# Spectral and dense layers on one core: the first chunk's residual summed in PSUM by TensorE, in place of the last tile's

## The chip, the cores and the metric

The kernel runs on one core of a Trainium2 chip. The metric is the device time of one execution in microseconds (us), as the median of several runs. A core has five engines that run their own instruction streams and meet at semaphores: TensorE (PE, matmuls), VectorE (DVE), ScalarE (ACT), GpSimd (POOL) and SyncE (SP, here only an issuer of DMAs). TensorE reads SBUF and writes PSUM, which has 8 banks of 512 fp32 values per partition.

## What is computed

The reference applies two kinds of layer in turn, twice, each with a residual, to x of 2048 rows by 1024 columns in bf16:

```python
def _A_ref(x, w_r, w_i):
    B, S, D = x.shape
    X = rfft2(x.astype(jnp.float32), axes=(-2, -1))
    X = X * (w_r + 1j * w_i)
    return irfft2(X, s=(S, D), axes=(-2, -1)).astype(jnp.bfloat16)

def _B_ref(x, w1, b1, w2):
    h = jnp.einsum("bsd,df->bsf", x, w1) + b1
    sp = jnp.log1p(jnp.exp(-jnp.abs(h))) + jnp.where(h > 0, h, jnp.zeros_like(h))
    return jnp.einsum("bsf,fd->bsd", h * jnp.tanh(sp), w2)

x = A_x
x = x + _A_ref(_layernorm(x, axis=-1), A_w_r, A_w_i)
x = x + _B_ref(_layernorm(x, axis=-1), B_w1, B_b1, B_w2)
x = x + _A_ref(_layernorm(x, axis=-1), A_w_r, A_w_i)
x = x + _B_ref(_layernorm(x, axis=-1), B_w1, B_b1, B_w2)
```

S is 2048, D is 1024 and F, the inner width of the dense layer, is 3584. `_layernorm` subtracts the row's mean and divides by the root of its variance.

## The kernel before

**State.** The residual stream x stays in SBUF as `XS`, sixteen tiles of 128 rows by 1024 columns in bf16. `IDENT` is a 128x128 identity. The PSUM is one tensor `PS` of eight banks. A small planner in Python orders everything: `op`, `group` and `dma` put instructions on an engine's list and work out its waits from `Res` objects, one for each tile or bank. A reader waits for the writers, a writer for the writers and readers. The program order on each engine is the order of the calls. A `Res` after `begin()` takes writes to its parts, each of which waits only for what was there before. `copy` lists the bank that it reads among its writes, so it counts as a writer of it.

**Transform layer (`layer_A`).** The two-dimensional transform is done as chains of matmuls by tables (`s1`, `s2`, `s3`, then `i1`, `i2`), in eight groups. At the end each group's result goes to DRAM and comes back turned (`u_turn`, `u_back`, `u_last`) as `UT`, with a `Res` for each of four quarters of its 128 row slots. While the last rows come, TensorE runs `spin`, matmuls of width 512 whose result nobody reads (line 905, 26 of them on bank 0). `load_w1` then starts the six first blocks of the dense weights.

**Start of the dense layer (`layer_B`).** The transform's last step is a matmul for each row slot of `UT` with a slice of `MT` (`i4`, line 968). With `lo` 0 and `nb` 4 it gives tiles 0 to 3 (32 columns per slot, 16 slots to a bank), with `lo` 4 and `nb` 12 the other twelve tiles (96 columns per slot). `i4_out` takes the sums out of PSUM. At lines 1146 to 1151, for each quarter `u`: `i4` into banks 2u and 2u+1; VectorE adds tiles 0 and 1 to `XS` (line 990); ScalarE copies tiles 2 and 3 to a buffer `YC` (line 568); VectorE takes statistics of a quarter of tiles 0 and 1 (`stats_quarter`, lines 472 and 474). The other twelve tiles come in pieces of up to 15 slots (`rest`, copied to `YS`, mostly by ScalarE). Then `root` (ScalarE's root at line 432, VectorE's reciprocal at 434), `apply` (the normalisation, line 512), transposes on TensorE (line 1024) with VectorE's copy (line 1029), and the first product `mm1` with the activation Mish on ScalarE (lines 1058 and 1062). Tiles are taken in chunks of four, and the first chunk's `mm1` at first in halves of 256 rows, with `rest` pieces between (lines 1169 to 1175). `residual` (line 1137) adds `YC` to tiles 2 and 3 and `YS` to tiles 4 to 15, on VectorE.

**End of the dense layer.** `mm2` forms the second product, 28 matmuls for each half of a tile (line 1079), and VectorE adds it to `XS` (line 1087). In the first dense layer each finished tile is normalised at once for the second transform. Tiles 0 to 14 go through DRAM (`xn_store`, `xr_load`). Of tile 15 the second half is done otherwise: an identity matmul puts the residual into PSUM first (line 1077), the product is summed on top of it, and `finish_last` takes the statistics and normalises straight from PSUM, in two halves. `xr_direct` then moves the tile as sixteen DMAs, one for each half and column block, on SP, ScalarE and POOL in turn: rows 0 to 3 after the first half, 4 to 15 after the second. The matmuls of the next `s1` (line 629) wait for the first eight of them in half 0, and later for half 1. A spin of 24 fills the wait (line 1245).

Three lines that are easy to miss, the planner's rule in `copy` and the order of the queues:

```python
return self.op(prog, fn, reads=reads, writes=writes, parts=parts)
...
self.copy(prog or self.act, at(staged.ap), src, [], rb, parts=[staged.res])
...
prog = (self.sp, self.act, self.pool)[i % 3]
```

Of the kernel before, what the change touches and what calls it, by code (L numbers as in the profile page):

```python
# [7 lines left out]
P = 128  # L8
# [171 lines left out]
class KB:  # L180
# [352 lines left out]
    def xr_direct(self, j, b, rows):  # L533

        for i in rows:
            half, h = i // 8, i % 8
            n = slice(64 * half, 64 * half + 64)
            prog = (self.sp, self.act, self.pool)[i % 3]
            self.dma(prog, self.XR.ap[row_of(j, h):row_of(j, h) + 1, n, :], b.ap[n, h * P:(h + 1) * P], f"xd{half}{prog.name}",
                     reads=[b.res], parts=[self.r_xr[2 * half]])  # L540

    def finish_last(self, bank):


        j, dve, ps = 15, self.dve, self.PS[:, bank, :]
        rb, r = self.r_bank[bank], self.r_mv[15]
        self.op(dve, lambda e: e.bn_stats(self.BN[:, j, 6:12], ps), reads=[rb], parts=[r])
        self.op(dve, lambda e: e.bn_aggr(self.MV[:, j, :], self.BN[:, j, :]), reads=[r], writes=[r])
        self.root(j, 1)
        b = self.xn_out[0]  # L550
        assert not b.unread
        mean, rs = self.MV[:, j, 0:1], self.RS[:, 2, j:j + 1]
        b.res.begin()
        for h in range(2):
            src = ps if h else self.XS[:, j, 0:512]
            self.op(dve, lambda e, h=h, src=src: e.tensor_scalar(b.ap[:, 512 * h:512 * h + 512], src, mean, rs, op0=ALU.subtract, op1=ALU.mult),
                    reads=[rb if h else self.r_xs[j], r, self.r_rs[j]], parts=[b.res])
            self.xr_direct(j, b, range(4, 16) if h else range(4))
        self.copy(self.act, self.XS[:, j, 512:1024], ps, [], [rb, self.r_xs[j]])
# [125 lines left out]
    def layer_A(self, li):  # L685
# [219 lines left out]
        self.spin(26, 0)  # L905
# [55 lines left out]

    def i4(self, lo, nb, u0, n, bank):

        w = 8 * nb
        k = 512 // w
        fns = []
        for l in range(n):
            fns.append(lambda e, l=l: e.matmul(self.PS[:, bank + l // k, l % k * w:(l % k + 1) * w], self.UT.ap[:, u0 + l, :],  # L968
                                               self.MT[:, 8 * lo:8 * lo + w], start=True, stop=True))
        self.group(fns, reads=self.r_ut[u0 // 32:(u0 + n - 1) // 32 + 1] + [self.r_mt], writes=self.r_bank[bank:bank - (-n // k)])  # L970

    def i4_out(self, lo, nb, u0, n, bank, staged=None, prog=None, tiles=None):
# [3 lines left out]
        t0, tn = tiles or (0, nb)  # L976

        for b0, m, i in ((0, n // k, k), (n // k, 1, n % k)):
            if not m or not i:
                continue  # L980
            src = self.PS[:, bank + b0:bank + b0 + m, 0:i * w].rearrange("p b (i c) -> p c b i", c=w)[:, 8 * t0:8 * (t0 + tn)]
            l = slice(u0 + b0 * k, u0 + b0 * k + m * i)
            rb = self.r_bank[bank + b0:bank + b0 + m]

            def at(ap):
                return ap.rearrange("p n (h l) -> p (n h) l", l=P)[:, :, l].rearrange("p c (b i) -> p c b i", i=i)
            if staged is None:
                j = slice(lo + t0, lo + t0 + tn)
                xs = at(self.XS[:, j, :])
                self.op(self.dve, lambda e, src=src, xs=xs: e.tensor_tensor(xs, src, xs, ALU.add), reads=rb, parts=self.r_xs[j])  # L990
            else:

                self.copy(prog or self.act, at(staged.ap), src, [], rb, parts=[staged.res])
# [10 lines left out]
    def layer_B(self, li, last):  # L1004
# [63 lines left out]
        def mm2(c, t, h):  # L1068
# [5 lines left out]

            summed = not last and (j, h) == (15, 1)
            if summed:
                fns.append(lambda e: e.matmul(PS[:, bank, :], self.IDENT[:], self.XS[:, j, 512:1024], start=True, stop=False))
            for i, ft in enumerate(range(NF)):
                fns.append(lambda e, i=i, ft=ft: e.matmul(  # L1079
                    PS[:, bank, :], at.ap[:, ft, t * P:(t + 1) * P], W2[ft].ap[:, h * 512:(h + 1) * 512],  # L1080
                    start=(i == 0 and not summed), stop=(i == NF - 1)))
            self.group(fns, reads=ra + r_w2 + ([self.r_xs[j], self.r_ident] if summed else []), writes=[self.r_bank[bank]])
            if summed:
                self.finish_last(bank)
                return
# [9 lines left out]
            else:  # L1095
# [4 lines left out]
                self.xn_store(j, self.apply(j, out=True))  # L1100
# [13 lines left out]
        YC = self.alloc("YC", self.ob["XT1"], [2, self.D])  # L1114
        YC.res.begin()
        xn = {}
        for j in range(2):
            self.r_xs[j].begin()

# [15 lines left out]
        def residual(j):  # L1135
            y, i = (YS, j - 4) if j > 3 else (YC, j - 2)
            self.op(dve, lambda e: e.tensor_tensor(self.XS[:, j, :], self.XS[:, j, :], y.ap[:, i, :], ALU.add),
                    reads=[y.res], writes=[self.r_xs[j]])
# [7 lines left out]
        for u in range(4):  # L1146
            self.i4(0, 4, 32 * u, 32, 2 * u)
            self.i4_out(0, 4, 32 * u, 32, 2 * u, tiles=(0, 2))
            self.i4_out(0, 4, 32 * u, 32, 2 * u, staged=YC, tiles=(2, 2))
            for j in range(2):  # L1150
                self.stats_quarter(j, u)
        rest(0)
        self.root(0, 2)
# [3 lines left out]
        self.spin(6, 7)  # L1157
        for j in range(2):
            transposed(0, j, xn[j])
        rest(3)  # L1160
        self.warm(ACT.Mish)
        at_tiles(0)
        for j in (2, 3):
            residual(j)
# [4 lines left out]
        for fg in range(4):  # L1169
            mm1(0, fg, 0, mid=turns(0, 2, 3) if fg == 3 else ())  # L1170
            rest(3)
            if fg == 2:
                rest(6, 10, dve)
        mm1(0, 0, 1)
        rest(3, 13)
# [108 lines left out]
```

## Time and profile before

| quantity | value |
|---|---|
| median of 3 runs | 1019.48 us (1019.28 to 1019.52) |
| profiled execution, its own time | 1019.28 us |
| span of the profiled execution | 1017.5 us |
| mean granted TensorE clock | 0.996 |
| TensorE line 1079 (`mm2`), 1756 matmuls | 385.7 us busy, 379 ns each |
| TensorE line 1058 (`mm1`), 1950 matmuls | 389.3 us busy, 358 ns each |
| VectorE line 990 (add of tiles 0 and 1), 8 | 5.4 us busy, 678 ns each |
| VectorE line 472 (quarter statistics), 16 | 6.1 us busy, 413 ns each |
| ScalarE line 568 at 128x512, 8 | 4.8 us busy, 597 ns each |
| TensorE line 646 (spin), 84 | 18.9 us busy, 379 ns each |

Times inside the execution count from the first instruction of the span. A row's mean is the length of one instruction from start to end. Matmuls overlap, so a run of them takes less than count times mean: 24 spins of 379 ns took 5.34 us. In the chain of work that ended last, each piece is followed by what it released. "Idle before" names what an engine waited for. A granted clock of 0.5 means that TensorE ran at half rate.

### The profile page before, as it was taken

Reading aid. Unit: us, or ns where it says so; the run is one execution under the profiler, and the core shown is the slowest. Engines: PE = TensorE matmul, PEld = TensorE weight load, DVE = VectorE, ACT = ScalarE, POOL = GpSimd, SP = SyncE. Lnnn points to the kernel's source line nnn. Section 1 sums busy time; section 2 is a strip of 40 time slices with the busy share of each in tenths; the row PEclk is TensorE's granted clock in tenths of the full one; section 3 lists DMA queues with packets and bytes.
Section 4 is the critical chain, followed back from the end, with each engine's and each line's share of the span. In section 5 each row is a group of like instructions: output and inputs, shape, how many; then the busy total and the mean of one; then the engine's idle time right before and its main releaser. Section 6 shows DMA issues by size and latency. Waiting matters only on the chain.

```text
span 1017.5 us, 13734 instructions
## 1 busy us (share of the span) xinstructions
PE 956.8 (94%) x5780; PEld 507.8 (50%) x5866; DVE 327.8 (32%) x679; ACT 347.9 (34%) x483; POOL 81.5 (8%) x114
## 2 busy tenths in 40 slices
PE   0799799999999999999999978999999999999998
PEld 0577475444444444444446757644444444444443
DVE  6797469002344000033346836830011100000111
ACT  7798383430000344300019847543200024330000
POOL 4651000000000000002521100000000000000000
PEclk9999999999999999999999999999999999999999
DMA  9979823562111220001922974246411212100000
GB/s 285 244 221 319 209 64 108 178 211 74 46 46 33 73 83 21 1 21 72 207 63 74 241 187 134 91 159 206 127 26 46 74 52 75 50 1 11 21 26 27
DMA packets 154205, 107.00 MB, mean 105 GB/s; under 512 B 74448, under 2 KB 133664, under 8 KB 154144
## 3 DMA queue, kind: packets, MB, share of 16 engines
q1 hardware_dynamic: 143056, 78.61, 27.5%
q0 software_dynamic: 8912, 25.84, 8.9%
q10 hardware_dynamic: 2176, 1.66, 0.5%
q8 instruction: 47, 0.77, 0.3%
q14 instruction: 14, 0.11, 0.0%
HBM read 80.85 MB, written 20.71 MB: 100 GB/s over the span
## 4 chain that ended last, share of the span: by engine, by line
PE 86%; DMA 4%; DVE 3%; SPq 3%; ACT 3%; issue 1%; POOL 0%; ACTq 0%; DVEq 0%; POOLq 0%
PE PS L1079 38%; PE PS L1058 37%; SPq L249 3%; PE PS L789 2%; PE PS L715 2%; PE PS L810 2%; DMA ARENA<-in_A_w_i_dram 1%; PE PS L968 1%; DMA ARENA<-c_bt 1%; DMA ARENA<-u_scratch 1%; ACT ARENA L568 1%; PE PS L828 1%; PE PS L1024 1%; PE PS L761 1%; ACT ARENA L796 1%
## 5 line engine op out<-in xcount | busy, mean ns | idle before, releaser
L1058 PE MATMUL PS<-ARENA 128*128 128x512 bf16 (+1 forms) x1950 | 389.3, 358 | 2.5 <-DVE ARENA L1029 0.6
L1079 PE MATMUL PS<-ARENA 128*128 128x512 bf16 x1756 | 385.7, 379 | 1.9
L1062 ACT ACTIVATE ARENA<-PS,B 128x512 bf16<-128x512 f32 (+1 forms) x248 | 158.9, 645 | 410.9 <-PE PS L1058 410.6
L1058 PEld LDWEIGHTS PS<-ARENA 128*128 128x128 bf16 x1984 | 192.9, 98 | 193.7 <-DVE ARENA L1029 1.6
L1079 PEld LDWEIGHTS PS<-ARENA 128*128 128x128 bf16 x1792 | 175.3, 98 | 211.3
L1087 DVE TENSOR_TENSOR XS<-PS,XS 128x512 bf16<-128x512 f32 x63 | 43.6, 692 | 581.3 <-PE PS L1079 581.3
L460 DVE BATCH_NORM_STATS2 BN<-XS 128x6 f32<-128x512 bf16 x99 | 64.0, 675 | 6.0 <-DMA XS<-in_A_x_dram 4.8
L568 ACT ACTIVATE ARENA<-PS 128x1440 bf16<-128x1440 f32 (+3 forms) x26 | 28.0, 1095 | 28.4 <-DVE XS L990 24.8
L249 POOL DMA_DIRECT2D xn_scratch<-ARENA x12 | 6.5, 541 | 375.8 <-DVE ARENA L512 375.8
L789 PE MATMUL PS<-ARENA 128*128 128x256 bf16 x256 | 32.4, 273 | 4.1 <-DVE ARENA L778 3.2
L796 ACT ACTIVATE ARENA<-PS 128x1024 bf16<-128x1024 f32 x32 | 33.1, 1054 | 7.0 <-PE PS L789 7.0
L432 ACT ACTIVATE RS<-MV,EPS 128x2 f32<-128x2 f32 (+2 forms) x5 | 1.5, 298 | 97.4 <-DVE MV L463 84.4
L715 PE MATMUL PS<-FD,ARENA 128*128 128x256 bf16 (+1 forms) x256 | 31.8, 271 | 2.4 <-ACT ARENA L635 1.2
L767 ACT ACTIVATE ARENA<-PS 128x1024 bf16<-128x1024 f32 x32 | 32.5, 1044 | 4.5 <-PE PS L763 4.5
L789 PEld LDWEIGHTS PS<-ARENA 128*128 128x128 bf16 x256 | 24.3, 98 | 11.8 <-DVE ARENA L778 5.5
L771 DVE TENSOR_TENSOR ARENA<-ARENA 128x1024 bf16<-128x1024 bf16 x32 | 22.0, 689 | 20.4 <-ACT ARENA L767 20.3
L810 PE MATMUL PS<-ARENA,BD 128*128 128x256 bf16 x192 | 25.9, 280 | 2.3 <-ACT ARENA L796 2.3
L838 ACT ACTIVATE ARENA<-PS 128x1024 bf16<-128x1024 f32 x26 | 26.8, 1066 | 2.9 <-PE PS L810 2.9
L715 PEld LDWEIGHTS PS<-FD,ARENA 128*128 128x128 bf16 x256 | 24.4, 98 | 6.5 <-DVE ARENA L637 1.4
L512 DVE TENSOR_SCALAR ARENA<-XS,MV,RS 128x1024 bf16<-128x1024 bf16 x47 | 25.3, 563 | 0.9
L968 PE MATMUL PS<-MT,ARENA 128*128 128x32 bf16 (+1 forms) x512 | 21.2, 195 | 4.0 <-ACT ARENA L568 2.0
L750 ACT ACTIVATE ARENA<-PS 128x1024 bf16<-128x1024 f32 x22 | 22.9, 1058 | 3.1 <-PE PS L715 3.1
(83 smaller groups left out, 519.8 us busy)
## 6 DMA issues: line engine op xcount, KB each, us to landing
ARENA<-in_B_w_dram SPq DMA_DIRECT2D x56, 512.0 KB, 4.0
ARENA<-in_B_w_dram SPq DMA_DIRECT2D x56, 256.0 KB, 4.3
u_scratch<-ARENA SPq DMA_DIRECT2D x14, 512.0 KB, 3.7
ARENA<-u_scratch SPq DMA_DIRECT2D x14, 512.0 KB, 6.1
w_scratch<-ARENA POOLq DMA_DIRECT2D x8, 512.0 KB, 6.5
ARENA<-w_scratch POOLq DMA_DIRECT2D x8, 512.0 KB, 5.0
out_dram<-XS SPq DMA_DIRECT2D x16, 256.0 KB, 2.0
ARENA<-xn_scratch POOLq DMA_DIRECT2D x15, 256.0 KB, 9.5
```

Source lines behind the costliest of these rows:

```text
L249: return eng.dma_start(out_ap, in_ap).then_inc(ds.sem, 16)
L460: self.op(self.dve, lambda e: e.bn_stats(self.BN[:, j, 6 * h:6 * h + 6], self.XS[:, j, 512 * h:512 * h + 512]), reads=[self.r_xs[j]], part ...
L568: fn = (lambda e: e.activation(dst, src, ACT.Copy)) if scale is None else \
L715: fns.append(lambda e: e.matmul(dst, at(r), FD[:, t:t + n], start=start, stop=stop))
L767: self.op(act, lambda e: e.activation(x.ap.rearrange("p a b -> p (a b)"), ps, ACT.Copy, scale=SIG), reads=banks, writes=[x.res])
L789: fns.append(lambda e, c=c, part=part: e.matmul(ps[:, c * 256:(c + 1) * 256], yk.ap[:, part, c * P:(c + 1) * P], t[:, (128, 0)[part]:(384, ...
L796: self.op(act, lambda e: e.activation(v.ap[:, :, i, :], src, ACT.Copy), reads=banks, parts=[v.res])
L810: fns.append(lambda e, dst=dst, part=part, c=c: e.matmul(dst, BD[:, c:c + P], mov(kd, part), start=(part == 0), stop=(part == 1)))
L1058: fns.append(lambda e, db=db, bank=bank, fl=fl: e.matmul(PS[:, bank, 0:w], wb.ap[:, db, fl * P:(fl + 1) * P], x.ap[:, db, tok], start=(db ...
L1062: self.op(act, lambda e, bank=bank, ft=ft: e.activation(at.ap[:, ft, tok], PS[:, bank, 0:w], ACT.Mish, bias=self.B1[:, ft:ft + 1]), reads= ...
L1079: fns.append(lambda e, i=i, ft=ft: e.matmul(PS[:, bank, :], at.ap[:, ft, t * P:(t + 1) * P], W2[ft].ap[:, h * 512:(h + 1) * 512], start=(i ...
L1087: self.op(dve, lambda e: e.tensor_tensor(xs, PS[:, bank, :], xs, ALU.add), reads=[self.r_bank[bank]], writes=[self.r_xs[j]])
```

## The change

There are two parts. Tile 15 loses its own treatment: `finish_last` and the identity matmul go, its second half is added by VectorE and normalised as a whole like other tiles, and `xr_direct` issues all sixteen DMAs after that. The first chunk is given the identity matmul instead: `residual_first` puts `XS` of tiles 0 to 3 into the eight banks, with 8 identity matmuls of width 512, after a spin of 8 (before: a spin of 26). `i4` for these tiles then sums on top. ScalarE copies the sums of tiles 0 and 1 to `XS` (`out_first`), and VectorE takes only the statistics; the sums of tiles 2 and 3 follow, three copies on ScalarE and one on VectorE, ahead of the root in the program. `YC` and its two adds go, so does the spin of 6 on bank 7, and the `rest` pieces are dealt out anew: two before the normalisation, none between transposes and `mm1`, and three small ones on VectorE. Both dense layers have the change at their start; only the first had the tile 15 treatment.

```diff
--- before.py
+++ after.py
@@ -530,33 +530,15 @@
         self.dma(self.pool, self.XR.ap[row_of(j, 0):row_of(j, 7) + 1:4, :, :], self.xn_d[j].rearrange("n (h l) -> h n l", l=P), f"xl{j % 4}",
                  reads=[self.r_xnd[j]], parts=self.r_xr[1:3])
-    def xr_direct(self, j, b, rows):
-        for i in rows:
+    def xr_direct(self, j, b):
+        b.unread = False
+        for i in range(16):
             half, h = i // 8, i % 8
             n = slice(64 * half, 64 * half + 64)
             prog = (self.sp, self.act, self.pool)[i % 3]
             self.dma(prog, self.XR.ap[row_of(j, h):row_of(j, h) + 1, n, :], b.ap[n, h * P:(h + 1) * P], f"xd{half}{prog.name}",
                      reads=[b.res], parts=[self.r_xr[2 * half]])
-    def finish_last(self, bank):
-        j, dve, ps = 15, self.dve, self.PS[:, bank, :]
-        rb, r = self.r_bank[bank], self.r_mv[15]
-        self.op(dve, lambda e: e.bn_stats(self.BN[:, j, 6:12], ps), reads=[rb], parts=[r])
-        self.op(dve, lambda e: e.bn_aggr(self.MV[:, j, :], self.BN[:, j, :]), reads=[r], writes=[r])
-        self.root(j, 1)
-        b = self.xn_out[0]
-        assert not b.unread
-        mean, rs = self.MV[:, j, 0:1], self.RS[:, 2, j:j + 1]
-        b.res.begin()
-        for h in range(2):
-            src = ps if h else self.XS[:, j, 0:512]
-            self.op(dve, lambda e, h=h, src=src: e.tensor_scalar(b.ap[:, 512 * h:512 * h + 512], src, mean, rs, op0=ALU.subtract, op1=ALU.mult),
-                    reads=[rb if h else self.r_xs[j], r, self.r_rs[j]], parts=[b.res])
-            self.xr_direct(j, b, range(4, 16) if h else range(4))
-        self.copy(self.act, self.XS[:, j, 512:1024], ps, [], [rb, self.r_xs[j]])
     def pair(self):
         i = self.npair % 4
@@ -902,7 +884,8 @@
             else:
                 i2(g, h)
                 u_turn(g, h)
-        self.spin(26, 0)
+        self.spin(8, 0)
+        self.residual_first()
         if li == 0:
             self.op(self.pool, lambda e: e.tensor_copy(self.B1[:], self.B1h[:]), reads=[self.r_b1h], writes=[self.r_b1])
         self.w1_buf = [self.alloc(f"W1_{i}", (self.W1_OFF + i * 4096, 140 * K + (i - 4) * 4096)[i > 3], [8, 256]) for i in range(6)]
@@ -959,6 +942,16 @@
         i = 2 * g % 8
         self.dma(self.pool, self.w_d[g], self.wt_pair(i), f"ws{g % 4}", reads=[w.res for w in self.WT[i:i + 2]], writes=[self.r_wd[g]])
+    def residual_first(self):
+        for b in range(8):
+            out = self.PS[:, b, :].rearrange("p (l c) -> p c l", c=32)
+            xs = self.XS[:, 0:4, :].rearrange("p n (h l) -> p (n h) l", l=P)[:, :, 16 * b:16 * b + 16]
+            self.group([lambda e, out=out, xs=xs: e.matmul(out, self.IDENT[:], xs, start=True, stop=False)],
+                       reads=self.r_xs[0:4] + [self.r_ident], writes=[self.r_bank[b]])
+        for r in self.r_xs[0:4]:
+            r.begin()
     def i4(self, lo, nb, u0, n, bank):
         w = 8 * nb
@@ -966,31 +959,30 @@
         fns = []
         for l in range(n):
             fns.append(lambda e, l=l: e.matmul(self.PS[:, bank + l // k, l % k * w:(l % k + 1) * w], self.UT.ap[:, u0 + l, :],
-                                               self.MT[:, 8 * lo:8 * lo + w], start=True, stop=True))
+                                               self.MT[:, 8 * lo:8 * lo + w], start=lo > 0,
+                                               stop=lo > 0 or l % k == k - 1))
         self.group(fns, reads=self.r_ut[u0 // 32:(u0 + n - 1) // 32 + 1] + [self.r_mt], writes=self.r_bank[bank:bank - (-n // k)])
-    def i4_out(self, lo, nb, u0, n, bank, staged=None, prog=None, tiles=None):
+    def out_first(self, u, t, prog):
+        b = slice(2 * u, 2 * u + 2)
+        src = self.PS[:, b, :].rearrange("p b (i c) -> p c b i", c=32)[:, 8 * t:8 * t + 16]
+        dst = self.XS[:, t:t + 2, :].rearrange("p n (h l) -> p (n h) l", l=P)[:, :, 32 * u:32 * u + 32]
+        self.copy(prog, dst.rearrange("p c (b i) -> p c b i", i=16), src, [], self.r_bank[b], parts=self.r_xs[t:t + 2])
+    def i4_out(self, lo, nb, u0, n, bank, staged, prog):
         w = 8 * nb
         k = 512 // w
-        t0, tn = tiles or (0, nb)
         for b0, m, i in ((0, n // k, k), (n // k, 1, n % k)):
             if not m or not i:
                 continue
-            src = self.PS[:, bank + b0:bank + b0 + m, 0:i * w].rearrange("p b (i c) -> p c b i", c=w)[:, 8 * t0:8 * (t0 + tn)]
+            src = self.PS[:, bank + b0:bank + b0 + m, 0:i * w].rearrange("p b (i c) -> p c b i", c=w)
             l = slice(u0 + b0 * k, u0 + b0 * k + m * i)
-            rb = self.r_bank[bank + b0:bank + b0 + m]
-            def at(ap):
-                return ap.rearrange("p n (h l) -> p (n h) l", l=P)[:, :, l].rearrange("p c (b i) -> p c b i", i=i)
-            if staged is None:
-                j = slice(lo + t0, lo + t0 + tn)
-                xs = at(self.XS[:, j, :])
-                self.op(self.dve, lambda e, src=src, xs=xs: e.tensor_tensor(xs, src, xs, ALU.add), reads=rb, parts=self.r_xs[j])
-            else:
-                self.copy(prog or self.act, at(staged.ap), src, [], rb, parts=[staged.res])
+            dst = staged.ap.rearrange("p n (h l) -> p (n h) l", l=P)[:, :, l].rearrange("p c (b i) -> p c b i", i=i)
+            self.copy(prog, dst, src, [], self.r_bank[bank + b0:bank + b0 + m], parts=[staged.res])
     def load_w1(self, after=()):
@@ -1071,18 +1063,11 @@
             bank = 3 + no[0] % 3
             no[0] += 1
             fns = []
-            summed = not last and (j, h) == (15, 1)
-            if summed:
-                fns.append(lambda e: e.matmul(PS[:, bank, :], self.IDENT[:], self.XS[:, j, 512:1024], start=True, stop=False))
             for i, ft in enumerate(range(NF)):
                 fns.append(lambda e, i=i, ft=ft: e.matmul(
                     PS[:, bank, :], at.ap[:, ft, t * P:(t + 1) * P], W2[ft].ap[:, h * 512:(h + 1) * 512],
-                    start=(i == 0 and not summed), stop=(i == NF - 1)))
-            self.group(fns, reads=ra + r_w2 + ([self.r_xs[j], self.r_ident] if summed else []), writes=[self.r_bank[bank]])
-            if summed:
-                self.finish_last(bank)
-                return
+                    start=(i == 0), stop=(i == NF - 1)))
+            self.group(fns, reads=ra + r_w2, writes=[self.r_bank[bank]])
             xs = self.XS[:, j, h * 512:(h + 1) * 512]
             self.op(dve, lambda e: e.tensor_tensor(xs, PS[:, bank, :], xs, ALU.add),
                     reads=[self.r_bank[bank]], writes=[self.r_xs[j]])
@@ -1097,7 +1082,11 @@
                     self.scales(j, 1)
                 else:
                     self.root(j, 1)
-                self.xn_store(j, self.apply(j, out=True))
+                b = self.apply(j, out=True)
+                if j == 15:
+                    self.xr_direct(j, b)
+                else:
+                    self.xn_store(j, b)
         w2v = self.w2.rearrange("(ft fp) d -> fp ft d", fp=P)
         W2 = [None] * NF
@@ -1111,12 +1100,7 @@
         YS = self.alloc("YS", self.o["YS"], [12, self.D])
         YS.res.begin()
-        YC = self.alloc("YC", self.ob["XT1"], [2, self.D])
-        YC.res.begin()
         xn = {}
-        for j in range(2):
-            self.r_xs[j].begin()
         def at_tiles(c):
             off = self.ob[f"AT{c}"]
             AT[c] = self.alloc(f"AT{c}", off, [NF, 512])
@@ -1133,9 +1117,8 @@
             self.i4_out(4, 12, u0, n, bank, staged=YS, prog=prog)
         def residual(j):
-            y, i = (YS, j - 4) if j > 3 else (YC, j - 2)
-            self.op(dve, lambda e: e.tensor_tensor(self.XS[:, j, :], self.XS[:, j, :], y.ap[:, i, :], ALU.add),
-                    reads=[y.res], writes=[self.r_xs[j]])
+            self.op(dve, lambda e: e.tensor_tensor(self.XS[:, j, :], self.XS[:, j, :], YS.ap[:, j - 4, :], ALU.add),
+                    reads=[YS.res], writes=[self.r_xs[j]])
         def turns(c, *ts):
             return [lambda t=t: transposed(c, t, xn[4 * c + t]) for t in ts]
@@ -1145,23 +1128,21 @@
         for u in range(4):
             self.i4(0, 4, 32 * u, 32, 2 * u)
-            self.i4_out(0, 4, 32 * u, 32, 2 * u, tiles=(0, 2))
-            self.i4_out(0, 4, 32 * u, 32, 2 * u, staged=YC, tiles=(2, 2))
+            self.out_first(u, 0, act)
             for j in range(2):
                 self.stats_quarter(j, u)
+        for u in range(4):
+            self.out_first(u, 2, (act, act, act, dve)[u])
+        self.root(0, 2)
         rest(0)
-        self.root(0, 2)
         rest(3)
         for j in range(2):
             xn[j] = self.apply(j)
-        self.spin(6, 7)
         for j in range(2):
             transposed(0, j, xn[j])
-        rest(3)
         self.warm(ACT.Mish)
         at_tiles(0)
         for j in (2, 3):
-            residual(j)
             self.stats_dve(j)
         self.scales(2, 2)
         for j in (2, 3):
@@ -1169,10 +1150,10 @@
         for fg in range(4):
             mm1(0, fg, 0, mid=turns(0, 2, 3) if fg == 3 else ())
             rest(3)
-            if fg == 2:
-                rest(6, 10, dve)
+            if fg:
+                rest(6, (10, 10, 3)[fg - 1], dve)
         mm1(0, 0, 1)
-        rest(3, 13)
+        rest(3)
         assert self.u0 == P
         for j in range(4, 8):
             residual(j)
```

## The prediction

> **What bounds the kernel now.** I read the page first: engines' busy time, then the chain that ended last by engine and line.
>
> ```profile
> span 1017.5 us, 13734 instructions
> PE 956.8 (94%) x5780; PEld 507.8 (50%) x5866; DVE 327.8 (32%) x679; ACT 347.9 (34%) x483; POOL 81.5 (8%) x114
> PE 86%; DMA 4%; DVE 3%; SPq 3%; ACT 3%; issue 1%; POOL 0%; ACTq 0%; DVEq 0%; POOLq 0%
> ```
>
> TensorE is the bound, 86% of the chain, and nearly all of that is the two matmul lines of the dense layers, which the change leaves alone. Time can only be won or lost where the chain leaves TensorE, so I read the chain in order of time at the three places that the diff touches: the start of each dense layer (two, some 492 us apart) and the passage from the first dense layer into the second transform. The first dense layer starts so:
>
> ```profile
> 112.00 3.94 DMA ARENA<-u_scratch
> 116.18 0.96 PE PS L968 x32
> 117.17 0.70 DVE XS L990
> 117.90 0.75 DVE BN L472 x2
> ...
> 122.03 1.86 ACT ARENA L568 x2
> 123.89 0.19 ACT RS L432
> 124.10 0.18 DVE RS L434
> 124.31 0.56 DVE ARENA L512
> 124.91 1.07 PE PS L1024 x16
> ```
>
> Columns are start, length, work. The rows land, TensorE sums quarter 0 in 0.96 us, and then VectorE holds the chain: add (L990) and two statistics (L472), four times over, 117.17 to 123.34. ScalarE's four copies of tiles 2 and 3 each begin when the add of their quarter ends (the waits view gives 24.8 us for eight of them); `copy` counts as a writer of the bank and so waits for its reader. Last, the root (L432) sits behind the copy of the first `rest`. TensorE's own order shows what it does meanwhile:
>
> ```profile
> 110.17 5.56 PE L646 MATMUL PS<-FD,BD 128*128 128x512 bf16 x25 [1.55 <-DVE ARENA L836]
> 116.18 3.03 PE L968 MATMUL PS<-MT,ARENA 128*128 128x32 bf16 x115 [0.45 <-DMA ARENA<-u_scratch]
> ```
>
> The spin ahead of the rows is filler that ends at 115.7, just before they land; the sums of all four quarters are ready by about 119.9, so VectorE's chain, not TensorE's, makes the 8.1 us from 116.18 to the normalisation at 124.31. The second dense layer repeats it (608.52 to 616.64, 8.1 us). The passage between the layers:
>
> ```profile
> 515.93 0.70 DVE XS L1087
> 516.68 0.39 PE PS L1077
> ...
> 523.14 0.71 DVE BN L547
> ...
> 524.65 1.14 DVE ARENA L556 x2
> 525.82 0.75 ACTq L249
> 526.59 2.25 DMA ARENA<-ARENA
> ```
>
> The identity matmul (L1077) waits for the add of the tile's first half: TensorE idles 0.79 us. After the last matmul come statistics, root and two normalisations, then sixteen row DMAs on three queues; TensorE restarts at 529.19 when ScalarE's third lands.
>
> **What the Trainium skill says.** (1) "PSUM — Partial Sum Buffer", The four PSUM rules: a seed other than zero should go in through an identity matmul that begins the accumulation. The change does that; the trace has one such seed (L1077), at 390 ns like other 512-wide matmuls. (2) "SBUF — State Buffer", Door 1: non-contiguous PSUM access "significantly slows down matmuls", with lines of two fp32 values. The new matmuls write with a step of 32 elements. No matmul of this trace does, so it neither agrees nor disagrees. (3) "TensorE: Matmul & The Clock Gate", Part 1: the clock halves after a window of about 3.4 us with little work, and windows don't start with the kernel. The trace agrees on the length (3.41 us); what counts as little is seen here:
>
> ```profile
> 102.06:105.47 3.41, 1.35 (x11) 0.98 (x12) 0.85 (x3) 2.05 (x2) 0.00 (x0) 1.00 1.01 265
> 105.47:108.89 3.42, 3.15 (x27) 2.01 (x25) 0.23 (x1) 1.02 (x1) 0.00 (x0) 0.50 1.23 212
> 119.13:122.54 3.41, 2.12 (x47) 1.71 (x43) 3.27 (x9) 1.70 (x4) 0.00 (x0) 1.00 1.05 302
> 607.23:610.64 3.41, 2.12 (x85) 2.15 (x86) 1.10 (x3) 0.41 (x1) 0.00 (x0) 1.00 0.34 67
> 610.64:614.06 3.42, 3.11 (x71) 2.80 (x67) 3.35 (x9) 1.38 (x3) 0.00 (x0) 0.50 0.69 191
> ```
>
> The second number is TensorE's busy time, the third from the end the granted clock. 1.35 busy of 3.41 was followed by half clock; 2.12 was once and once not.
>
> **The change part by part.**
>
> *Seeding.* Spins fall from 26 to 8 and eight identity matmuls follow. The spins start near 109.95 and run at 0.216 us (24 in 5.34 us at the other spin). Eight end at 111.7; eight seeds at the same rate end at 113.4, at double price 115.2. The rows land at 115.94 (608.38 in the second layer, with spins from 601.4), so seeds cost nothing up to 0.53 us each in the first layer and 0.65 us in the second; the cover is the DMA wait. Bounds: 0.216 (plain rate) and, from the page's wording without a number, several times that; I take 0.43.
>
> *First chunk.* The add leaves VectorE (4 x 0.67). ScalarE copies tiles 0 and 1 (0.60 as L568 at 128x512), then VectorE does only statistics. Quarters come from TensorE every 0.85 us, a copy takes 0.60 and statistics 0.75, so each is ready before the next quarter. Fourth quarter at 119.85 (116.18 + 128 x 0.0264 + the 0.30 gap seen there): copy to 120.47, statistics and aggregates 1.31 (as 122.03 to 123.34) to 121.80. ScalarE now has three copies of tiles 2 and 3 ahead of the root; back to back they step 0.49, so it is free at 121.83, level with the statistics. Root to 122.13. The fourth such copy is VectorE's, ahead of its reciprocal: 0.70 (between L990's 0.67 and L572's 1.16 for 960, scaled), to 122.5. Normalisation starts at 122.7 against 124.31: 1.6 gained. In the second layer, without the 0.30 gap: sums end 3.44 after start, normalisation 6.3 after it against 8.12: 1.8.
>
> *What follows.* Transposes start 0.6 later and the first mm1 2.0 after them, as before: 125.3 for 126.91. The six spins at bank 7 and one `rest` between transposes and mm1 go; two `rest` now run in the wait for the normalisation. Then ScalarE: two `rest` copies of 1.46 from 122.2, table load and dummy 1.48, free at 126.45, when half of the first mm1 is done (126.35). From mm1 on TensorE needs, by the rows of before, five mm1 halves at 1.75, five `rest` of fifteen at 0.65, 0.43 twice, 0.13, and 0.9 of transposes: 13.9. Before it took 14.56 with stalls (0.58 for ScalarE's copy at 131.88, 0.38 for VectorE's at 136.75). Now ScalarE's copies come free 0.1 to 0.7 ahead of need; VectorE has lost two adds of 0.68 and gained copies of 1.16 and about 0.5, and I find one stall of 0.35, the second bank-6 copy ahead of transposes 2 and 3. The stage ends at 139.5 for 141.47: 1.95 gained in the first layer, 2.2 in the second. Weights don't stop it: six blocks of 512 KB come at some 290 GB/s from 118.2, the first by 120 and all by 130, and mm1 takes a new one every 2.4 us. Later waits (residuals 4 to 7) hang on the last `rest` copy and move with it.
>
> *Last tile.* No seed, no wait: the second half's matmuls start at 515.73 instead of 516.90, ending at 521.95: 1.17 earlier. Then add, statistics, root, one normalisation as tile 14 had (509.95 to 512.74: 2.79), all data at 524.76. Before, four rows went at 525.09 and the rest from 525.80. All sixteen DMAs now start together: six on SP, five each on ScalarE and POOL, 0.62 to 0.67 apart, so ScalarE's third starts at 526.06, before 526.59: 0.53 gained, all the way to TensorE. If the queues were slower this would shrink to nothing, not become a loss of over 0.5. ScalarE's copy into XS (0.60) goes, off the path. The 24 spins end about 527.3 and restart is at 528.7.
>
> *Clock.* With six spins gone, the window 119.13 to 122.54 would hold about 1.5 busy (0.45 of sums, 1.05 of `rest`), near the 1.35 that was punished. Half clock across transposes and the first mm1 costs 16 x 0.05 plus part of 0.87, less ScalarE's slack: 0.6. Windows fall as they fall; I take one in two layers.
>
> Sum: 1.95 + 2.2 + 0.53 - 0.6 = 4.1 off the span of 1017.5. The profiled execution took 1019.28, 1.8 around its span; the median is 0.2 above it. So 1019.48 - 4.1 = **1015.4**.
>
> **Rivals.** *A, as above*, 1013.8 to 1016.2, chance 0.55. *B, clock and covers*: half clock at both starts (1.2) and a further stall of 0.5 on a ScalarE copy in each, since its slack is 0.1 at the first Mish: gain 2.5, 1017.0 (1016.2 to 1017.4), chance 0.23. For it: the busy windows above. Against: half clock leaves the sums' pace unchanged (26 per half us after 610.65, 27 before). *C, the chain moves to ScalarE*: its three copies ahead of the root and the copies after it hold the loop, or other waits take the place; some 1.5 gained, 1018.0, chance 0.15. *D, slower: seeds at a stride.* With price r each, rows wait 8r - 4.2 and 8r - 5.2; 16r - 9.4 equals the gain of 4.7 without a clock loss at r = 0.88, four times the plain price. At eight times, 1.75, it costs 18.6: 1033.4. For it: the page's sentence; against: a step to the next line costs one half of a two-value line, so double is my reading. Chance 0.07.
>
> The range from 1013.8 to 1018.0 leaves out D, C's upper half and a little of A. A measurement of this kernel tells about 0.2% (2.0 us) from no change: A and B are faster, C two fifths so and the rest within, D nearly all slower: 0.84, 0.10, 0.06.
>
> **What would show it.** Seeds: rows of identity matmuls of 128x512 ahead of the rows' landing, done before it; the step between them is r. First chunk: normalisation 6.4 us after the first sum instead of 8.1, with ScalarE copies at its head and no VectorE add. Loop: first dense-only mm1 23.3 after the first sum, not 25.3. Last tile: no idle at 516, restart near 528.7. Clock: half-clock stretches after 122. Wrong would be the prediction if the sums start late, if ScalarE's copies run far over 0.60, or if the stretch from normalisation to the full-width mm1 lengthens by what its start gains.

## The result and the profile after

| | before | after |
|---|---|---|
| median, runs on record | 1019.5 us (1019.28 to 1020.71, 4 runs) | 1015.41 us (1014.96 to 1016.21, 4 runs) |
| ratio, 95% interval | | 0.9958 [0.9941, 0.9976] |
| profiled execution, span | 1019.28 us, 1017.5 | 1014.96 us, 1013.1 |
| the same kernels later, in many runs | 1018.5 us (1015.75 to 1023.05, 59 runs) | 1017.64 us (1013.64 to 1021.5, 22 runs) |
| ratio there, 95% interval | | 0.9994 [0.9985, 1.0004] |

The forecast was 1015.4 us. The runs on record gave that, but with many more runs the kernel proved to vary by several microseconds from one execution to the next, and the gain was then 0.9 us by the medians, 0.6 by the ratio, whose interval reaches from a gain of 1.5 to a loss of 0.4. So there are two things to explain: what the change does in the trace, and why so little of it is left on average.

The page of the changed kernel, the lines that answer to those of before:

```profile
span 1013.1 us, 13670 instructions
PE 952.0 (94%) x5749; PEld 506.0 (50%) x5833; DVE 323.9 (32%) x673; ACT 348.7 (34%) x484; POOL 81.6 (8%) x114
PE 87%; DMA 4%; SPq 3%; DVE 2%; ACT 2%; issue 1%; POOL 0%; ACTq 0%; DVEq 0%
```

VectorE's share of the chain fell from 3% to 2%, ScalarE's from 3% to 2%. The chain at the first dense layer's start (start, length, work; L961 is `i4`, L550 `copy`, L1016 the transposes):

```profile
110.00 4.54 DMA ARENA<-u_scratch
...
114.67 2.70 PE PS L961 x96
117.37 0.02 issue
117.39 1.58 ACT XS L550 x3
118.98 0.05 issue
119.02 2.58 PE PS L961 x30
121.60 0.77 PE PS L1016 x8
```

The adds and statistics of VectorE are gone from it at this start. In their place stand three ScalarE copies and then the two `rest` pieces on TensorE, which hold the transposes. At the second start the chain still goes through VectorE, with statistics, the fourth copy of tiles 2 and 3 and the normalisation, but no add:

```profile
610.28 0.44 DVE BN L472
...
611.59 0.55 DVE XS L554
...
612.24 0.56 DVE ARENA L512
```

TensorE's timeline says why the thirty `rest` matmuls of the first start take so long; the last line is the same work at the second dense layer's start:

```profile
108.92 3.61 PE L950 MATMUL PS<-XS,IDENT 128*128 128x512 bf16 x8
...
114.67 2.68 PE L961 MATMUL PS<-MT,ARENA 128*128 128x32 bf16 x96 [1.36 <-DMA ARENA<-u_scratch]
119.02 2.58 PE L961 MATMUL PS<-MT,ARENA 128*128 128x96 bf16 x30 [1.67 <-ACT XS L550]
121.40 1.40 PE L1016 MATMUL PS<-IDENT,ARENA 128*128 128x128 bf16 x16
...
611.28 1.45 PE L961 MATMUL PS<-MT,ARENA 128*128 128x96 bf16 x30 [1.67 <-ACT XS L550]
```

The eight seeds took 3.61 us and ended 2.0 us before the last rows. After the sums TensorE waited 1.67 us for ScalarE to empty banks. Then the thirty `rest` matmuls took 2.58 us at the first start and 1.45 at the second: half clock was granted from 115.3 to 122.1 in the first case, and from 606.8 to 610.2, over before the `rest` pieces, in the second. The passage between the layers:

```profile
518.86 0.70 DVE XS L1072
...
521.08 0.56 DVE ARENA L512
521.64 0.02 issue
521.66 0.57 ACTq L249
522.23 0.03 issue
522.26 0.87 ACTq L249
523.13 0.03 issue
523.16 2.25 DMA ARENA<-ARENA
```

No wait for an identity matmul is left, add, statistics and normalisation stand in line on VectorE, and the third of ScalarE's row DMAs is still what TensorE waits for.

Cutting each trace at the same points shows where the 4.4 us between the two profiled spans came from. "Sum" is the start of the last of the 128 first-chunk sums, "dense" that of the first `mm1` after the last `rest`, "restart" the first matmul of the second transform; the times are read from TensorE's timeline, in us.

| stretch | before | after | gained |
|---|---|---|---|
| start of the span to first sum point | 119.81 | 117.17 | 2.64 |
| first start, sum to dense | 21.66 | 21.11 | 0.55 |
| dense to restart (the passage in it) | 387.72 | 387.47 | 0.25 |
| restart to second sum point | 82.58 | 83.68 | -1.10 |
| second start, sum to dense | 22.03 | 19.96 | 2.07 |
| dense to the end | 383.68 | 383.68 | 0.00 |

The stretches that the change edits give 2.87. The other 1.54 lies in stretches in which the rows for the sums come. Over all traces, late seeds (e8) apart, the first of these runs from 117.2 to 121.3, in no order that follows the edits. The second does follow them: 82.55 to 82.60 in the three traces without seeds (before, e2, e3), 82.97 to 83.90 in the seven with seeds behind eight spins (one of them, e1, has half clock in the stretch), 82.45 to 82.72 in the three with seeds behind thirteen. So the 1.10 lost there may be a cost of the change too; why the rows come later then is not shown. In the first one, half clock had fallen on the kernel before from 105.5 to 108.9, where 12 matmuls of line 810 took 2.48 us and 16 of line 828 1.03, where the same work took 1.48 and 0.62 in the trace of the experiment c_after: 1.4 us that have nothing to do with the edit.

### The profile page after: what moved, and what is told of

Its sections match the earlier page's. It is cut to its first block, busy times and chain, and to the rows that moved or that the text cites. A ratio compares the mean times of both kernels' runs of the same rounds, so it can differ in the third digit from the quotient of the medians.

```text
span 1013.1 us, 13670 instructions
## 1 busy us (share of the span) xinstructions
PE 952.0 (94%) x5749; PEld 506.0 (50%) x5833; DVE 323.9 (32%) x673; ACT 348.7 (34%) x484; POOL 81.6 (8%) x114
## 4 chain that ended last, share of the span: by engine, by line
PE 87%; DMA 4%; SPq 3%; DVE 2%; ACT 2%; issue 1%; POOL 0%; ACTq 0%; DVEq 0%
PE PS L1067 38%; PE PS L1050 38%; SPq L249 3%; PE PS L771 2%; PE PS L697 2%; PE PS L792 2%; PE PS L961 2%; DMA ARENA<-in_A_w_i_dram 1%; DMA ARENA<-u_scratch 1%; DMA ARENA<-c_bt 1%; DMA u_scratch<-ARENA 1%; PE PS L1016 1%; PE PS L743 1%; ACT ARENA L778 1%; PE PS L810 1%
## 5 line engine op out<-in xcount | busy, mean ns | idle before, releaser
L961 PE MATMUL PS<-MT,ARENA 128*128 128x32 bf16 (+1 forms) x512 | 21.4, 199 | 7.1 <-DMA ARENA<-u_scratch 3.8
L961 PEld LDWEIGHTS PS<-MT,ARENA 128*128 128x128 bf16 x512 | 20.0, 102 | 9.8 <-issue 4.5
```

## The experiments

Theory: the change shortens the chain from sums to normalisation by some 1.7 to 2 us at each start, and TensorE, idle for longer there, is then granted half clock on the work that follows, which takes much of it back. Rivals: the tile-15 part carries the gain; the new deal of the `rest` pieces carries it; the seeds' stride or their lateness matters. Each run was timed beside runs of the kernel before on the same chip; the medians of these lie between 1018.2 and 1018.5 us on all four chips, about 1 us under the 1019.5 from which the first expectations count. The table of stretches (one trace for each kernel, times in us; the ratio is to the kernel before):

| kernel | first start, sum to dense | second start | dense to restart | mean clock | time, ratio |
|---|---|---|---|---|---|
| e1_chunk_only | 20.76 | 20.77 | 387.76 | 0.993 | 1017.54, 0.9992 [0.9982, 1.0001] |
| e2_tile_only | 21.53 | 22.11 | 387.52 | 1.000 | 1019.0, 1.0001 [0.9988, 1.0014] |
| e3_redeal_only | 24.23 | 24.14 | 387.74 | 0.990 | 1023.35, 1.005 [1.0035, 1.0066] |
| e4_tile_seed_last | 20.96 | 21.19 | 387.11 | 0.995 | 1017.25, 0.9988 [0.9978, 0.9998] |
| c_after | 22.39 | 20.91 | 387.48 | 0.993 | 1017.64, 0.9994 [0.9985, 1.0004] |
| e5_old_deal | 21.70 | 21.13 | 387.54 | 0.995 | 1018.69, 1.0002 [0.9994, 1.001] |
| e6_spin13 | 22.62 | 21.12 | 387.49 | 0.995 | 1017.08, 0.9984 [0.9972, 0.9995] |
| e7_plain_seeds | 21.30 | 20.90 | 387.48 | 0.991 | 1016.87, 0.9988 [0.9979, 0.9997] |
| e8_late_seeds | 22.63 | 19.95 | 387.49 | 0.996 | 1020.95, 1.0028 [1.0014, 1.0041] |
| e10_kept_warm | 19.97 | 19.97 | 387.50 | 1.000 | 1013.41, 0.9953 [0.9939, 0.9967] |
| e11_best | 19.95 | 19.98 | 387.11 | 1.000 | 1013.42, 0.9952 [0.9939, 0.9965] |
| e12_gap_spins | 19.95 | 19.96 | 387.48 | 0.996 | 1014.53, 0.9961 [0.9949, 0.9974] |

**e1_chunk_only and e2_tile_only**, one part each.

```diff
 # e1: the changed kernel, with finish_last, xr_direct and mm2 of before
+            summed = not last and (j, h) == (15, 1)
 # e2: the kernel before, with xr_direct and mm2 of the changed kernel
-            summed = not last and (j, h) == (15, 1)
```

> The changed kernel, but with tile 15 treated as before (identity matmul at the head of its group, normalised from PSUM in two halves): the first-chunk part of the change alone. Theory (the chain at the two starts of the dense layers is shortened): nearly the whole gain stays, 1015.7 to 1016.0 us. Rival (the passage between the layers, with TensorE's 1.2 us of hold-up ahead of tile 15's last group, carries it): 1018 or more.

> The kernel before, with only tile 15 treated as in the changed kernel: the other part alone. Prediction's step: 0.53 gained, 1019.0 us; by the trace of the changed kernel, where the third of ScalarE's row DMAs started only 0.24 earlier against the tile's first add, about 1019.2. Rival (all of TensorE's 1.17 counts): 1018.3.

Measured: 1017.54 and 1019.0, neither clear of no change, so the expectation for the first part failed. By the stretches the first part gains 0.9 and 1.3 at the starts, against 1.7 and 2.1 where the clock is full; the second gains 0.20 in the passage and nothing else. So by the traces the first part is where the gain is, in some half of the size that was expected, and the rival that tile 15 carries it is out.

**e3_redeal_only**, the new order without the shorter chain.

```diff
-        rest(0)
         self.root(0, 2)
+        rest(0)
...
-        self.spin(6, 7)
-        rest(3)
-            if fg == 2:
-                rest(6, 10, dve)
+            if fg:
+                rest(6, (10, 10, 3)[fg - 1], dve)
```

> The kernel before, with VectorE's add and tile 15 as before, and only the order of the changed kernel: root ahead of the first rest copy, two rest pieces ahead of the normalisation, no spin of 6, three pieces on VectorE. Theory: the root comes 0.43 earlier, but VectorE still has the two residual adds (1.36) ahead of its PSUM copies and holds TensorE at the second of them, so 0.2 to 0.5 for each dense layer, 1018.5 to 1019.1 us. Rival (the new deal of the rest pieces is what gains): 1016.5 or less.

Both expectations failed: it is 5 us slower. The timeline shows where:

```profile
125.17 1.60 PE L1024 MATMUL PS<-IDENT,ARENA 128*128 128x128 bf16 x16 [2.34 <-DVE ARENA L512]
127.55 3.60 PE L1058 MATMUL PS<-ARENA 128*128 128x256 bf16 x16 [0.79 <-DVE ARENA L1029]
```

TensorE waited 2.34 us for the normalisation, where before it had the spin, and then its first sixteen `mm1` matmuls took 3.60 us instead of the 1.92 of before, at half clock granted from 125.5 for 6.8 us. This run put the clock at the head of the suspects.

**e4_tile_seed_last**, a version in which the tile-15 seed doesn't wait.

```diff
-            if summed:
-                fns.append(lambda e: e.matmul(PS[:, bank, :], self.IDENT[:], self.XS[:, j, 512:1024], start=True, stop=False))
...
+            if summed:
+                self.group([lambda e: e.matmul(PS[:, bank, :], self.IDENT[:], self.XS[:, j, 512:1024], start=False, stop=True)],
+                           reads=[self.r_xs[j], self.r_ident], writes=[self.r_bank[bank]])
```

> The changed kernel, with tile 15 normalised from PSUM in two halves as before, but with the identity matmul at the end of its group instead of the head, so that it no longer waits for the add of the first half. Theory: the matmuls start at once, the identity matmul costs 0.22 at the end, and all that follows comes 0.95 earlier than before: 0.95 below the first-chunk part alone and about 0.7 below the changed kernel, 1014.7 us. Rival (the row DMAs' issue hides it): no better than the changed kernel, 1015.4.

```profile
520.64 0.39 PE PS L1092
...
522.56 1.15 DVE ARENA L556 x2
523.71 0.02 issue
523.73 0.75 ACTq L249
524.48 0.03 issue
524.51 2.28 DMA ARENA<-ARENA
```

The seed is issued at the end and waits for nothing. The passage is 0.61 shorter than before and 0.36 shorter than in the changed kernel, half of the 0.7 expected; the time, 1017.25 where 1014.7 was expected, can't show so little.

**c_after**, the changed kernel again, and three edits of it beside it.

> The changed kernel as it is, once more, beside the same runs of the kernel before as the three that follow. By the traces so far its stages gain 0.25 in the passage, 2.1 from the last first-chunk sum to the full-width mm1 where the clock stays full, and 0.6 to 0.9 where half clock falls on the transposes: 1.5 to 4.5 us in all, about 3 on average, a ratio near 0.997. If the first figure of 4.1 us is the change's own, 0.996 again.

It came out below the weak end of what was expected, at 0.9994. Its windows view from the `rest` pieces to the second `mm1` (length, then TensorE's busy time; the granted clock is the third number from the end):

```profile
119.63:121.19 1.56, 1.56 (x31) 1.45 (x31) 1.49 (x6) 1.35 (x3) 0.00 (x0) 0.85 1.22 306
121.19:123.86 2.67, 1.89 (x18) 1.62 (x17) 1.84 (x4) 2.65 (x3) 0.00 (x0) 0.50 1.16 293
123.86:127.25 3.39, 3.39 (x16) 2.39 (x17) 3.21 (x9) 1.31 (x3) 0.00 (x0) 0.50 1.16 326
```

Transposes and all of the first `mm1` ran at half clock: 1.6 us more for that `mm1` alone, and 2.43 from sum to dense against the 19.96 of the clean start, the second one of the changed kernel's first trace.

**e5_old_deal, e6_spin13, e7_plain_seeds.**

```diff
 # e5
+        rest(3)
         self.warm(ACT.Mish)
...
-            if fg:
-                rest(6, (10, 10, 3)[fg - 1], dve)
+            if fg == 2:
+                rest(6, 10, dve)
 # e6
-        self.spin(8, 0)
+        self.spin(13, 0)
 # e7
-            out = self.PS[:, b, :].rearrange("p (l c) -> p c l", c=32)
+            out = self.PS[:, b, :].rearrange("p (c l) -> p c l", c=32)
```

> The changed kernel with the rest pieces dealt as before: one between transposes and mm1, one of ten on VectorE, a last one of 13 (the spin of 6 stays out, the root stays ahead). Theory: the new deal earned nothing (17.15 from normalisation to the full-width mm1 in both), and a rest in the gap between transposes and mm1 is free, 0.65 and more of TensorE's work taken out of the loop, with ScalarE's table load 1.35 later as the price: 0 to 0.8 us less for each dense layer than the changed kernel, 1 us less in all. Rival (the new deal belongs to the gain): 1 to 2 us more than the changed kernel.

Measured 1018.69, some 1 us over c_after, though the intervals of the two meet: the expectation failed and the rival's figure held. From first `mm1` to dense it took 15.01 us, against 14.54 in the changed kernel, because ScalarE's table load now comes after a third copy. So the new deal earns about 0.5 at each start once the chain is short.

> The changed kernel with 13 spins instead of 8 ahead of the seeds. Clock theory: TensorE idles 1.1 us less before the rows, half clock falls less often on transposes and the first mm1, 0.3 to 1.0 us less than the changed kernel. Cover theory: the seeds end 1.1 later, at 6.2 after the first spin; the last rows come 6.0 to 8.8 after it, so no loss over 0.2. Rival (idle time ahead of the rows doesn't matter to the clock later): equal to the changed kernel.

Measured 1017.08, by 0.6 less than c_after, within the intervals. Half clock still fell on both starts, now only behind the sums, from 120.6 and from 612.1:

```profile
119.02 1.45 PE L961 MATMUL PS<-MT,ARENA 128*128 128x96 bf16 x30 [1.67 <-ACT XS L550]
...
123.25 3.60 PE L1050 MATMUL PS<-ARENA 128*128 128x256 bf16 x16 [0.79 <-DVE ARENA L1021]
```

Filling the time ahead of the rows is not enough.

> The changed kernel, but the eight identity matmuls write their bank in plain order instead of with a step of 32 elements, so that the residual of tiles 0 to 3 goes to other columns: only the price of the stride is measured. Theory (the stride doubles the matmul): step 0.216 instead of 0.43, length 380 instead of 634 ns, 3.6 us of seeds become 1.9, and the time stays within 0.5 us of the changed kernel, since the wait for the rows covers both. Rival (the identity matmul reading XS in short runs is what is slow): step stays 0.43.

In this run the residual of tiles 0 to 3 is added to other columns than its own, so that only its time counts. The line view of the seeds, first in the changed kernel, then here (duration min/median/max in ns):

```profile
L950 PE MATMUL PS<-XS,IDENT x16: 602/634/634, 108.9 to 602.9; 128*128 128x512 bf16 x16
```

```profile
L950 PE MATMUL PS<-XS,IDENT x16: 379/379/390, 109.4 to 601.7; 128*128 128x512 bf16 x16
```

Plain seeds are as short as any 512-wide matmul, so the short runs that they read cost nothing and the stride of the writes makes them 634 ns. The step of the strided ones is (3.61 - 0.634)/7 = 0.425. The time fell by 0.8 against c_after, again within the intervals.

**e8_late_seeds**, 26 spins ahead of the seeds.

```diff
-        self.spin(8, 0)
+        self.spin(26, 0)
```

> The changed kernel with 26 spins ahead of the seeds, so that the seeds end 9.0 us after the first spin, where the last rows came 6.0 to 8.8 after it. Cover theory (seeds are free only while the rows are on their way): the sums begin up to 3 us later, the last first-chunk sum 1.5 to 2.5 later after the first spin at each start, 3 to 5 us in all, less what a busier TensorE saves of half clock (up to 2): 1 to 4 us more than the changed kernel. Rival (a seed can be late, since the last rows decide): no difference.

```profile
115.10 3.61 PE L950 MATMUL PS<-XS,IDENT 128*128 128x512 bf16 x8
118.50 3.40 PE L961 MATMUL PS<-MT,ARENA 128*128 128x32 bf16 x128
```

The sums follow on the seeds with no wait for a DMA: the cover is used up. 1020.95, 3.3 over c_after, as the cover theory had it.

**e10_kept_warm, e11_best and e12_gap_spins**, the direct test of the clock.

```diff
-        self.spin(8, 0)
+        self.spin(13, 0)
...
             self.out_first(u, 0, act)
+            if u == 1:
+                self.out_first(0, 2, act)
...
-        for u in range(4):
+        self.spin(6, 0)
+        for u in range(1, 4):
             self.out_first(u, 2, (act, act, act, dve)[u])
...
             transposed(0, j, xn[j])
+        self.spin(3, 2)
 # e11: the same with tile 15 as in e4; e12: with spin(8, 0) and without spin(3, 2)
```

> The changed kernel with TensorE kept busy through the start of the dense layer: 13 spins ahead of the seeds, ScalarE's first copy of tiles 2 and 3 moved up behind its second copy of tiles 0 and 1 so that bank 0 comes free, six spins on it in the 1.67 us in which TensorE waited for ScalarE, and three spins on bank 2 in the 0.8 to 0.9 between transposes and mm1. Clock theory (half clock on rest, transposes and first mm1 is what the changed kernel loses, 0.6 to 2.6 us at each start): from the last first-chunk sum to the full-width mm1 20.0 to 20.3 at both starts, instead of 21 to 22.6, 2 to 3 us less than the changed kernel in all, about 1015.0 us. Rival (half clock comes from the sums themselves, 32 columns each, and falls anyway): equal to the kernel with 13 spins, about 1017.

```profile
119.08:120.88 1.80, 1.44 (x30) 1.29 (x31) 1.73 (x6) 1.37 (x3) 0.00 (x0) 1.00 1.19 305
120.88:122.88 2.00, 1.67 (x18) 1.11 (x20) 1.74 (x4) 1.98 (x3) 0.00 (x0) 1.00 1.22 294
122.88:124.64 1.76, 1.76 (x16) 1.58 (x17) 1.73 (x4) 1.61 (x3) 0.00 (x0) 1.00 1.16 297
```

The same stretch as in c_after, at full clock: first `mm1` 1.76 instead of 3.39. 19.97 at both starts, 1013.41 us, 4.2 less than the changed kernel's 1017.64, and only 1.7 between its lowest and highest run. The 4.2 are more than the 2 to 3 that were expected. Of the 4.7 between the profiled spans of c_after and e10, the two starts give 3.4, and 1.0 lies between restart and second sum point (83.46 and 82.45), where the rows come earlier again.

> As the one kept warm, and with tile 15's identity matmul at the end of its group and its normalisation from PSUM in two halves. The two gains are in different stages and should add: 0.4 less (the passage took 0.36 less with it in the trace), about 1014.6 us.

1013.42, no less than e10: the 0.39 of the passage is in the trace (387.11), but five runs that lie up to 1.2 apart don't show it.

> Of the kernel kept warm, only the middle piece: the moved copy and six spins on bank 0 between the sums and the rest pieces; 8 spins ahead of the seeds and none between transposes and mm1, as in the changed kernel. If the 1.67 us of idle after the sums is what brings half clock, most of the gain stays: 1013.4 to 1014.5 us, 19.9 to 20.3 from the last first-chunk sum to the full-width mm1. If the idle time ahead of the rows is the cause, about 1017, as the changed kernel on the same day.

```profile
115.69 3.48 PE L961 MATMUL PS<-MT,ARENA 128*128 128x32 bf16 x128 [0.54 <-DMA ARENA<-u_scratch]
119.24 1.24 PE L628 MATMUL PS<-FD,BD 128*128 128x512 bf16 x5
120.63 1.44 PE L961 MATMUL PS<-MT,ARENA 128*128 128x96 bf16 x30
...
124.40 1.92 PE L1050 MATMUL PS<-ARENA 128*128 128x256 bf16 x16 [0.92 <-DVE ARENA L1021]
```

Six spins between the sums and the `rest` pieces are enough: 19.95 and 19.96, although half clock was granted from 104.6, ahead of the first start, and from 606.4, over the sums of the second. 1014.53 us, and the ratio's interval lies clear of that of c_after. The moved copy was not run without the spins, but the changed kernel's clean start took the same 19.96, so the copy by itself earns nothing at full clock.

So what the changed kernel pays for is half clock that reaches past the sums. It can start ahead of the idle time after the sums, with the wait for the rows: of the four starts in its two traces, three were granted half clock before the sums had ended (from 115.3, 606.8 and 608.8). Once it ended with the sums and cost nothing, as at e12's second start; twice it lasted on, to 122.1 and 615.6. With a shorter wait ahead (e6) it came only after the sums, and with the idle time behind the sums filled (e12) no time is lost at either start. The 1.1 us between e12 and e10 are not taken apart; 0.7 of them could be the second rows (83.11 and 82.45).

## Why the prediction was right, and where it was not

That 1015.4 was met is luck. By many runs the kernel before lies 1.0 under its median on record and the changed kernel 2.2 above its own, so of the 4.1 us 0.9 is left. The parts fared as follows.

**Seeds.** Right: 0.43 taken, 0.425 measured, hidden in the wait; e7 shows the stride as the cause and e8 the end of the cover. The Trainium skill's sentence on non-contiguous PSUM access ("SBUF — State Buffer", Door 1) now has this case's number: the step doubles, from 0.216 to 0.425.

**First chunk.** Right. From the last sum to the normalisation before took 4.49 and 4.87 us by the traces; all traces with the seeds have 2.80 to 2.83 (2.85 was worked out).

**What follows.** Off by 0.35 for each start, the one stage in which the forecast gain did not come at all. From normalisation to dense I had 16.8; at full clock it is 17.15, as before the change (17.16). ScalarE's copy was said to come free 0.1 to 0.7 ahead of need. In e10 the copy ahead of the second `rest` of the loop ends at 127.14, and that `rest` starts at 127.20 where TensorE would have been ready at 127.03: 0.17 late. The stall of 0.35 for VectorE's copy was there, as 0.38 of idle; but idle time is counted from a matmul's end in the trace, and matmuls overlap, so from start to start it cost 0.54 (131.08 to 132.50 for eight `mm1` matmuls that take 0.88). Together the two starts gain 1.70 + 2.07 = 3.77 at full clock, not 4.15.

**Last tile.** Right in sign, half in size: 0.25 (0.20 in e2), not 0.53. Against the first half's add, VectorE's work on the last matmuls' result began 1.09 earlier (1.17 was worked out), and the data were ready 2.78 after that, as worked out (2.79). The larger part of the miss is ScalarE's issue of row DMAs: the third started 1.50 after the first (0.60 and 0.90 from start to start), not 1.30. It had taken 1.50 before as well (525.10 to 526.59), so starting all sixteen together won nothing there.

**Clock.** The mechanism is right and the size wrong: the term taken as 0.6, "one in two layers". Against 19.96 the changed kernel lost 1.15 and 0.00 in the trace on record, 2.43 and 0.95 in c_after, 1.34 and 0.94 in e7: about 2.3 in the mean of three. What I had not seen is that the 1.67 us of idle after the sums, made by the shorter chain itself, stands right behind the sums, so that a window with little work is made nearly every time (in c_after 1.74 us of work in the 3.41 from 117.30), and that half clock often lasts two windows, over the whole of the first `mm1` (1.6 us more in c_after) where I had counted a part of its first half. The Trainium skill's page "TensorE: Matmul & The Clock Gate", Part 1, is borne out on the windows: the half-clock stretches last 3.41 us or two or three times that (6.8 in c_after, 10.2 in e7), at places that differ from run to run.

The sum therefore was 3.77 + 0.25 - 2.3 = 1.7, still above c_after's 0.9 and the 1.5 at its interval's edge. A term that I had put at nothing, the rows of the second transform, would close most of the rest: 83.36 in the mean of the six traces with seeds behind eight spins, e1 apart, against 82.58 before, 0.8, which leaves 0.9. That the change causes it is not shown. The 4.1 on record needed a start without half clock, and 2.6 in the stretch ahead of the first sums. That is shown for the profiled execution by the table of stretches; for the other three runs on record, which have no trace, it is an inference. Rival B, half clock at both starts, with 1017.0, describes the changed kernel's long-run median of 1017.64 better than the case that I had put first. Rival C's figure, 1018.0, is nearer still, but its mechanism is not what the traces show: at full clock ScalarE's copies cost no more than worked out. Rival D was out by the seeds' price. What stays open: why a window is granted half clock or not, to a number.

## What to carry to other kernels

When an edit shortens a chain on other engines, look at what TensorE does in the time set free: if it idles behind small matmuls, put filler there, and give it a free bank to write to by emptying one early; here all the filler together was worth more than the edit by itself (4.2 us against 0.9, by medians). Cut the traces of both kernels at the same points before believing a difference of a few tenths of a per cent: at most two thirds of the difference between the two profiled spans was the change's. And take many runs, since four of each agreed among themselves and still missed the mean.

## What the runs showed of the hardware

Half clock hardly slows the sums of 32 columns: from start to start they take 0.025 us at full and 0.027 at half clock, 0.2 us more over 128 of them, while `mm1` at 256 columns takes 3.59 instead of 1.92 for sixteen. A matmul of 512 columns that writes PSUM with a step of 32 fp32 elements takes a step of 0.425 us, with a length of 634 ns, against 0.216 and 379. With TensorE kept busier, the spread of the runs shrank to 1.7 us (e10, 6 runs) and 1.2 (e11, 5 runs), from 3.9 in e3 and in e8 with 6 runs each and 7.9 in c_after with 22.
